# Half of one weight transfer cut into four 8-row pieces, each behind a tiny transfer, and 37 more filler products

## The chip, the cores and the metric

The kernel runs on one core of one Trainium2 chip. The metric is device time in microseconds (us), the median of several executions. A profile is one further execution. Its span (423.3 us for the kernel before) leaves out some 2 us that the device time has at its ends, so times on the profile's clock are compared only with one another. PE is the engine of the matrix products; its granted clock is the share of full speed at which it was allowed to run. POOL is the engine that issues the weight transfers, and the DMA share is the mean busy share of the core's sixteen DMA engines.

## The reference, cut to what matters

Linear attention makes `x`. A spectral step then mixes 64 frequencies of it, each with its own pair of 512 x 512 weight matrices, and a channel step ends it.

```python
def _moe_ref(x, w_r, w_i, w_ch):
    X = np.fft.rfft(x, axis=1)                       # x: 8 x 576 x 512
    Xr, Xi = (np.real(X[:, :64]), np.imag(X[:, :64]))
    Yr = np.einsum('bmd,mde->bme', Xr, w_r) - np.einsum('bmd,mde->bme', Xi, w_i)
    Yi = np.einsum('bmd,mde->bme', Xr, w_i) + np.einsum('bmd,mde->bme', Xi, w_r)
    ...                                              # the other frequencies are zero
    u = x + np.fft.irfft(Y, n=S, axis=1)
    return u + np.maximum(u @ w_ch, 0.0)
```

`w_r` and `w_i` hold 2 x 64 x 512 x 512 float32 values, 134 MB. The core reads all of them, each once, and that is the longest job of the kernel.

## The kernel before

The weights come in pairs of frequencies: pair p holds frequencies 2p and 2p+1. Each pair is two transfers issued from POOL, one from `w_r` and one from `w_i`, each of 64 rows of 32 KB. The transfer converts float32 to bfloat16, so a row is 16 KB on arrival (the trace of before has 16,384 bytes in a weight packet). Two buffers rotate. The last pair (31) comes in smaller pieces, so that little is left to do after the last one.

```python
    def w_load(p: int, half: int, pool, tag: str, bufs: int):
        if half == 0:
            w_in[p] = pool.tile([128, NDW, D], BF16, tag=tag, bufs=bufs, name=f"w{p}")
        two = (moe_w_r, moe_w_i)[half][2 * p : 2 * p + 2]
        pin(
            nc.gpsimd.dma_start(
                out=w_in[p][half::2], in_=two.rearrange("g (r dc) e -> (g r) dc e", dc=NDW)
            )
        )
    # ... cut: w_load_last, which loads pair 31 in pieces
```

`pin` keeps the written order of instructions. On PE each pair's products are followed by a number of fillers: products whose result nobody reads, there to keep the clock of PE up while it waits for weights.

```python
    def keep_warm(n: int):
        for _ in range(n):
            pin(nc.tensor.matmul(last_ps[0], id16, wch16[:, 0, :]))

    def mode_pair(p: int):
        # ... cut: the pair's products, their eviction and transposition
        keep_warm(FILL.get(p, 0))

    def last_pair():
        # ... cut: frequency 62
        keep_warm(6)
        kk = NM - 1
        y_last = psW.tile([128, NDC, 2 * B], F32, tag="P", bufs=2, name="y_last")
        # ... cut: 32 products with the last weights

    FILL = {**{p: 1 for p in range(20, 27)}, 27: 1, 28: 1, 29: 2, 30: 3}
```

## Time and profile before

| | before |
|---|---|
| median time, three runs | 424.95 us (424.81 to 425.3) |
| span of the profiled run, mean granted clock | 423.3 us, 0.788 |
| last landing of a weight | 389.70 us |
| from there to the end of the span | 33.6 us |

### The profile page before, as it was taken

What the parts mean: (1) busy time and instruction counts of PE and PEld (TensorE: products, weight loads), DVE (VectorE), ACT (ScalarE), POOL (GpSimd) and SP (SyncE); (2) the same over time, 40 slices, a digit from 0 to 9 for tenths busy, and PEclk for the clock granted to TensorE, in tenths of its full rate; (3) what the DMA queues carried; (4) which work ended last, traced back from release to release, by engine and by line L of the source; (5) the groups of instructions that cost most, each with busy time, mean ns of one, the idle gap of its engine ahead of it and who ended that gap; (6) DMA issues with size and microseconds to landing.
All of it is one profiled execution on the core that took longest, in us unless ns stands there. A gap on an engine that the chain in (4) does not pass through costs nothing.

```text
span 423.3 us, 7890 instructions
## 1 busy us (share of the span) xinstructions
PE 268.8 (63%) x3378; PEld 146.1 (35%) x3378; DVE 215.2 (51%) x447; ACT 161.4 (38%) x253; POOL 57.0 (13%) x99
## 2 busy tenths in 40 slices
PE   1358376778417645444344778869687785997992
PEld 0247355566202322222122323324243332463320
DVE  4599489994203453354444444445353424431793
ACT  4687588844202102000000244435253432330781
POOL 4222124210000100000000001100000000030000
PEclk9999889999755555555555598878898969899997
DMA  9999999999999999999999999999999999995697
GB/s 215 209 209 215 207 221 201 224 209 221 218 217 221 208 215 220 218 211 217 218 217 212 221 215 217 214 219 217 215 215 216 218 212 218 218 209 113 235 400 309
DMA packets 20802, 93.19 MB, mean 220 GB/s; under 512 B 2080, under 2 KB 11168, under 8 KB 16480
## 3 DMA queue, kind: packets, MB, share of 16 engines
q0 software_dynamic: 16512, 81.47, 93.8%
q1 hardware_dynamic: 4256, 11.22, 7.2%
q8 instruction: 26, 0.43, 0.4%
q14 instruction: 8, 0.07, 0.0%
HBM read 163.93 MB, written 9.44 MB: 410 GB/s over the span
## 4 chain that ended last, share of the span: by engine, by line
DMA 69%; PE 16%; DVE 4%; ACT 4%; issue 3%; POOL 2%; DVEq 0%; POOLq 0%; ACTq 0%
DMA w<-in_moe_w_i_dram 54%; DMA pick_sb<-row_pick 8%; PE P L442 7%; DMA k<-in_k_dram 7%; PE acc L735 3%; PE acc L774 2%; POOL w L119 2%; ACT ke L213 2%; ACT qT L249 1%; DVE ys L452 1%; DVE x L299 1%; PE yt L460 1%; ACT qe L213 1%; PE ya L653 0%; PE eps L676 0%
## 5 line engine op out<-in xcount | busy, mean ns | idle before, releaser
L442 PE MATMUL P<-w,xt_c 64*32 64x512 bf16 (+2 forms) x1000 | 51.7, 544 | 66.4 <-DMA w<-in_moe_w_i_dram 64.9
L452 DVE CAST ys<-P 128x512 f16<-128x512 f32 x32 | 22.1, 692 | 118.0 <-PE P L442 118.0
L454 ACT CAST ys<-P 128x512 f16<-128x512 f32 x31 | 18.2, 586 | 150.2 <-PE P L442 150.2
L119 POOL DMA_DIRECT2D w<-in_moe_w_r_dram x31 | 16.5, 534 | 245.1 <-PE P L442 105.9
L442 PEld LDWEIGHTS <-xt_c 64*32 64x32 bf16 (+2 forms) x1000 | 16.8, 128 | 84.7 <-DMA w<-in_moe_w_i_dram 51.1
L676 PE MATMUL eps<-wch,xTw 128*128 128x512 f16 x144 | 43.7, 434 | 0.0
L165 PEld LDWEIGHTS <-qT 64*128 64x128 f16 (+1 forms) x640 | 22.7, 123 | 52.9 <-issue 28.7
L657 DVE TENSOR_TENSOR x_main<-ya,x_main 128x512 f32<-128x512 f32 x32 | 22.0, 689 | 19.1 <-PE ya L653 18.9
L165 PE MATMUL num<-kv,qT 64*128 64x65 f16 (+1 forms) x320 | 13.4, 208 | 28.1 <-ACT kv L272 14.6
L659 ACT CAST x16w<-x_main 128x512 f16<-128x512 f32 x32 | 19.8, 618 | 25.0 <-DVE x_main L657 24.0
L684 ACT CAST E<-eps 128x512 f16<-128x512 f32 (+1 forms) x40 | 21.2, 541 | 11.2 <-PE eps L676 11.0
L165 PE MATMUL nw<-kv,qT 64*128 64x65 f16 (+1 forms) x320 | 19.0, 240 | 9.5 <-DVE x_tail L620 4.3
L460 PE MATMUL yt<-pick_sb,ys 128*128 128x16 f16 x252 | 11.7, 174 | 18.7 <-DMA pick_sb<-row_pick 12.1
L299 DVE TENSOR_TENSOR x<-num,rd 128x512 f16<-128x512 f32 x32 | 22.1, 692 | 1.1
L213 ACT ACTIVATE qe<-q 128x1152 f16<-128x1152 f16 (+1 forms) x16 | 17.8, 1156 | 10.5 <-DMA q<-in_q_dram 10.4
L249 ACT COPY qT<-qTp 128x1152 f16<-128x1152 f16 x16 | 19.7, 1298 | 0.2 <-PE qTp L242 0.2
L460 PEld LDWEIGHTS <-ys 128*128 128x128 f16 x252 | 9.7, 102 | 28.8 <-DVE ys L452 15.3
L242 PE MATMUL qTp<-id,qe 128*128 128x128 f16 x144 | 13.1, 264 | 10.0 <-DVE qe L226 9.5
L213 ACT ACTIVATE ke<-k 128x1152 f16<-128x1152 f16 x16 | 17.7, 1153 | 4.7 <-DMA k<-in_k_dram 4.7
L784 ACT ACTIVATE acc<-acc 128x512 f32<-128x512 f32 x34 | 18.1, 581 | 2.4 <-PE acc L735 1.5
L676 PEld LDWEIGHTS <-xTw 128*128 128x128 f16 x144 | 14.1, 110 | 12.6 <-issue 6.2
L119 POOL DMA_DIRECT2D w<-in_moe_w_i_dram x31 | 17.2, 555 | 4.8 <-DMA q<-in_q_dram 2.5
(114 smaller groups left out, 450.8 us busy)
## 6 DMA issues: line engine op xcount, KB each, us to landing
w<-in_moe_w_r_dram POOLq DMA_DIRECT2D x31, 1024.0 KB, 12.4
w<-in_moe_w_i_dram POOLq DMA_DIRECT2D x31, 1024.0 KB, 16.8
out_dram<-x_main SPq DMA_DIRECT2D x11, 512.0 KB, 4.8
k<-in_k_dram POOLq DMA_DIRECT2D x8, 576.0 KB, 12.7
v<-in_v_dram POOLq DMA_DIRECT2D x8, 576.0 KB, 14.8
q<-in_q_dram POOLq DMA_DIRECT2D x7, 576.0 KB, 12.7
out_dram<-x_main SPq DMA_DIRECT2D x6, 256.0 KB, 4.8
q<-in_q_dram SPq DMA_DIRECT2D x2, 576.0 KB, 4.4
```

Source lines behind the costliest of these rows:

```text
L119: nc.gpsimd.dma_start(out=w_in[p][half::2], in_=two.rearrange("g (r dc) e -> (g r) dc e", dc=NDW))
L165: mm = nc.tensor.matmul(num[hpo][orow, c0 : c0 + 65], qT[rows, hpp, h2, cols], kv_sb[rows, hpp, h2, :])
L213: pin(nc.scalar.activation(out=ev[:, c], in_=heads(nm, b, c), func=AF.Exp))
L249: nc.scalar.copy(out=qT[:, :, c * NJ : (c + 1) * NJ], in_=qT_ps.rearrange("p j x -> p x j"))
L299: nc.vector.tensor_tensor(out=dst.rearrange("p (o c d) -> p o c d", o=2, c=4), in0=nv[:, :, :, 0:64], in1=rden.unsqueeze(3).broadcast_to([ ...
L442: nc.tensor.matmul(P[c : c + n, :], xt_cols(dc, kk, n), w[rows, dc, :], start=(dc < NDC), stop=(dc >= n_dc - NDC), tile_position=(rows.sta ...
L452: pin(nc.vector.tensor_copy(out=st, in_=P))
L460: nc.tensor.matmul(yt_ps[:, ec, kk % 8, :], st[:, ec * 128 : ec * 128 + 128], pick_sb)
L657: pin(nc.vector.tensor_tensor(out=x, in0=acc, in1=x, op=ALU.add))
L659: pin(nc.scalar.copy(out=x16w[t], in_=x))
L676: nc.tensor.matmul(e_ps, xT[:, c, :], wch16[:, c, :], start=(c == 0), stop=(c == NDC - 1))
L684: pin(nc.scalar.copy(out=dst, in_=e_ps[:, cols]))
```

## The change

Eight of the sixteen DMA engines finish the weights some 3 us after the others (last landings of before at 388.36 to 389.70 us against 385.38 to 387.29). As I read the diff, the intent is to give the early half more rows of pair 20, so that all end together. Half of one transfer is sent as four transfers of 8 rows. The idea, as I read it, is that each of them goes to 8 engines and that the two halves take turns from one to the next; so a tiny transfer of 8 short rows stands before each, to use up the other half's turn. The fillers are set anew: 35 more behind the pairs from 20 on, and two more before the last products.

```diff
+    spare = const.tile([128, 2], F16, name="spare")[0:8]
 ...
+        rows_in = two.rearrange("g (r dc) e -> (g r) dc e", dc=NDW)
+        if (p, half) != (20, 0):
+            pin(nc.gpsimd.dma_start(out=w_in[p][half::2], in_=rows_in))
+            return
+        pin(nc.gpsimd.dma_start(out=w_in[p][half + 2 :: 4], in_=rows_in[1::2]))
+        for j in range(4):
+            for real in (0, 1):
+                if real:
+                    pin(nc.gpsimd.dma_start(out=w_in[p][half + 4 * j :: 16], in_=rows_in[2 * j :: 8]))
+                else:
+                    pin(nc.gpsimd.dma_start(out=spare, in_=moe_w_ch[0:8, 0:2]))
 ...
-        keep_warm(6)
+        keep_warm(8)
 ...
-    FILL = {**{p: 1 for p in range(20, 27)}, 27: 1, 28: 1, 29: 2, 30: 3}
+    FILL = {**{p: 4 for p in range(20, 27)}, 27: 7, 28: 1, 29: 8, 30: 5}
```

More of the change, by code (lines that the diff above doesn't have):

```diff
@@ L117, in w_load @@
         two = (moe_w_r, moe_w_i)[half][2 * p : 2 * p + 2]
-        pin(
-            nc.gpsimd.dma_start(
-                out=w_in[p][half::2], in_=two.rearrange("g (r dc) e -> (g r) dc e", dc=NDW)
-            )
-        )
+        rows_in = two.rearrange("g (r dc) e -> (g r) dc e", dc=NDW)
[9 more added lines that the diff above has]
+                    pin(nc.gpsimd.dma_start(out=spare, in_=moe_w_ch[0:8, 0:2]))
     def w_load_last(pool, tag: str, bufs: int):
```

## The prediction

The sum came to 424.95 + 6.4 - 0.55 = 430.8 us, less 0.5 for a shorter round trip: 430.3. The round trip of 2.6 us held 0.1 for waking POOL. The 6 and 2 rows an engine in (1), and with them the heavy and the light half in (2), are what the change intends if all four small transfers meet the same eight engines. That was assumed; the trace before does not show it.

> **What bounds the kernel now.** I read four views, in this order. First the page: its row of DMA shares and its chain that ended last.
>
> ```profile
> PEclk9999889999755555555555598878898969899997
> DMA  9999999999999999999999999999999999995697
> ...
> q0 software_dynamic: 16512, 81.47, 93.8%
> ...
> q8 instruction: 26, 0.43, 0.4%
> ...
> DMA 69%; PE 16%; DVE 4%; ACT 4%; issue 3%; POOL 2%; DVEq 0%; POOLq 0%; ACTq 0%
> ```
>
> The DMA engines are full from the first slice to the thirty-sixth; nine tenths of that is the queue that POOL issues to, which carries the weights. The chain is 69% DMA. Second, busy time by stage, around the end of the weights (columns: stretch, length, busy time and count of PE, PEld, DVE, ACT, POOL, then clock, DMA share, GB/s):
>
> ```profile
> 290.00:380.00 90.00, 71.89 (x739) 35.53 (x737) 36.56 (x69) 35.55 (x63) 12.17 (x23) 0.91 1.01 215
> 380.00:385.40 5.40, 3.81 (x35) 1.11 (x27) 0.69 (x1) 0.59 (x1) 0.00 (x0) 1.00 1.02 206
> 385.40:387.30 1.90, 1.90 (x16) 0.81 (x13) 1.32 (x2) 0.00 (x0) 0.00 (x0) 1.00 0.56 107
> 387.30:389.70 2.40, 1.74 (x31) 1.08 (x29) 0.00 (x0) 0.00 (x0) 0.00 (x0) 1.00 0.27 45
> 389.70:393.70 4.00, 3.60 (x20) 2.16 (x20) 1.09 (x3) 1.12 (x3) 0.33 (x1) 0.57 0.00 0
> ```
>
> The reader is to see that the share is full until 385.4 us and then falls in steps: about half the engines finish early while the rest work on. The trace keeps sixteen landings for each transfer, one an engine. Those of the very last weight piece are 385.38, .46, .63, .66, .81, 386.00, .17 (seven), 387.29 (one), 388.36, .54, .64, .69, .70, .76, .85 (seven) and 389.70. Eight engines are some 3 us behind. Why is in the trace too: the 25 instruction fetches of 16 KB before 389.7 (queue q8) take 0.89 to 0.98 us each, and their durations repeat with a period of eight, so they visit eight engines in turn, three each and a fourth for one. Third, the chain of waits at the end, and fourth, POOL's timeline where the changed load stands and at its last issue:
>
> ```profile
> 362.40 27.30 DMA w<-in_moe_w_i_dram x2
> 389.70 0.05 issue
> 389.75 0.30 PE y_last L504 x4
> 390.05 0.02 issue
> 390.07 0.24 DVE Y L510
> 390.31 0.05 issue
> 390.35 0.61 PE ypl L914 x4
> 390.96 0.85 PE zl L920 x4
> 391.81 0.85 PE z1l L920 x4
> ```
>
> ```profile
> 263.81 0.52 POOL L119 DMA_DIRECT2D w<-in_moe_w_r_dram  x1 [8.73 <-PE ya L653]
> 264.32 0.54 POOL L119 DMA_DIRECT2D w<-in_moe_w_i_dram  x1
> ...
> 393.37 0.57 POOL L929 DMA_DIRECT2D YZ_all<-last  x1 [15.62 <-ACT last L925]
> ```
>
> So everything waits for the last weight piece at 389.70, and what follows is a fixed tail of about 33 us. A transfer is 64 rows, four an engine; the trace's 16 KB packets (one row each) take 1.226 us, and the landings of successive transfers lie 4.85 us apart on each engine from start to end. There is no slack in this stream: any hole in it moves the end by its full length.
>
> [...] in an idle queue the issue at 393.37 had its first packet at 395.34 (1.97 us) and landed at 396.85 to 397.31. [...] a row's 32 KB read in 1.226 us is 26.7 GB/s,[...] a lone half gets no faster: the slow eight's steps over the last three small pieces are the fast eight's within 0.05 us. [...] stretches at half clock are multiples of 3.41 us, and one is 390.28 to 393.69, just behind the last weights.
>
> **The change part by part.** (1) Rows. Of pair 20's first transfer, half (32 rows) stays two an engine; the other 32 rows go as four transfers of 8 rows[...]. So eight engines get 6 rows, eight get 2: plus and minus 2 x 1.226 = 2.45 us. If the heavier half is the fast one, the ends become 387.8 to 388.6 for its seven, 389.74 for its eighth (387.29 + 2.45), and 385.9 to 387.25 for the others.
>
> (2) Waits, which the diff does not show and the built program does. All four tiny transfers write one tile, `spare`, so the second waits for the landing of the first, the third for the second, the fourth for the third: in the instruction order each carries a wait on the semaphore lane of the one before, at the count that includes it. POOL issues in order, so the real ones and the pair's second transfer stand behind these waits. The first tiny transfer lies in the queue behind pair 19 and the 32 rows. The slowest engine landed pair 19 at 272.05; plus 2.45 it reaches the tiny one at 274.5. At that moment the light half has nothing queued, and the heavy half only one row, which it has mostly finished. A round trip, by the issue at 393.37: 1.97 us to the first packet, about 0.5 from its end to the landing[...], so 2.6 (an estimate from that one transfer). Tiny issues then fall at 274.6, 277.2 and 279.8; the last real one at 280.3; the second transfer of the pair at 280.8, its packets from 282.8. Before, the slow engines started it at 275.1 to 276.5 (landings 275.49 to 276.90 less 0.4). The light half so loses 6.3 to 7.7 us. The heavy half gets its last row at 282.3 to 283.5 and goes on from there. All sixteen restart nearly together, so the old lag is wiped out whichever half was meant. From the end of that first transfer to the last landing an engine without fetches took 385.38 - 273.59 = 111.8 us, a fetching one 112.9. New end: heavy 283.9 + 111.8 to 112.3 = 395.7 to 396.2; light 283.2 + 112.9 = 396.1. Against 389.70: plus 6.4 us.
>
> (3) Eight more POOL issues of about 0.5 us: already inside (2).
>
> (4) 37 more fillers, 0.216 us apart at full clock: 8 us of PE, all behind waits for weights. The two added before y_last: the six end at 387.92, eight would end at 388.35, before y_last starts at 388.58. So no cost. Their possible gain: the window 386.86 to 390.28 held only about 1.1 us of streaming (columns over clock, added up from the trace) and was followed by half clock[...]. Two more fillers bring 1.5. With full clock ypl, zl and z1l (0.61 + 0.85 + 0.85) and the products after would take about 1.1 us less. But all of this moves by 6 us against the window's grid, so I count half: minus 0.55.[...]
>
> Sum: 424.95 + 6.4 - 0.55 = 430.8; as the round trip rests on one larger transfer and may be 2.3, I take off 0.5: 430.3 us.
>
> **Rivals.** (a) The balance works as meant and the waits cost nothing. The mean of the sixteen landings is 387.35, so 2.35 us is the most it can give; by (1) it gives 0 to 1.1, as the move overshoots. With the clock's 1.1: 422.8 to 425. For it: someone tuned these counts. Against it: three waits are in the built program, in a queue that is full before and empty behind them. (b) The heavy half is the slow one and there is no hole: 389.70 + 2.45 = 392.15, 427.4 us. (c) The hole is hidden by the load-ahead of two pairs. Against: at 263.81 the queue holds 5 to 8 us of work and the waits begin only when that is used up; PE waits for weights, never the other way for long. (d) A longer round trip, 3.3 us each, would bring 433.
>
> **Range and chances.** (2) dominates and I give it 85%: 428.5 to 432.5. Rivals (a) and (b) share the rest. Range 427.3 to 432.6. Over 2% slower needs 433.45, so rival (d): 8%. Over 2% faster needs 416.5, which no part can give: 1%.
>
> **What would show it.** Right: between about 274 and 283 us the DMA share falls well below 1; POOL has three issues spaced by 2.3 to 2.9 us ended by the landing of `spare`; the pair's second transfer is issued 15 us later than before; the last weights land near 396 with all engines within 1.5 us; the tail stays 33 us, less 1 if no half-clock window follows the last landing. Wrong: a DMA share of 1.0 through 270 to 290 and POOL issuing the nine transfers 0.5 us apart.

## More of the kernel before

One more view is needed to read the change: the busy time by stretch around the load that it touches. Its columns are the stretch, its length, busy time and count of PE, PEld, DVE, ACT and POOL, then the granted clock, the DMA share and GB/s.

```profile
270.00:274.00 4.00, 2.23 (x42) 1.40 (x42) 1.16 (x3) 1.02 (x2) 0.45 (x1) 1.00 0.96 205
274.00:276.00 2.00, 1.75 (x20) 0.80 (x19) 1.78 (x4) 1.23 (x3) 0.61 (x2) 1.00 1.08 229
276.00:278.00 2.00, 2.00 (x13) 0.79 (x11) 1.62 (x4) 1.08 (x2) 0.00 (x0) 1.00 1.04 221
278.00:283.00 5.00, 1.76 (x27) 0.61 (x33) 0.85 (x2) 1.72 (x3) 0.00 (x0) 0.80 1.02 218
```

The last but one column is what to read: the share is 1 throughout, give or take a few hundredths. The stream has no gap here, and POOL (the busy column with two and then no instructions) issues its next transfers long before they are needed.

## The result and the profile after

| | before | after |
|---|---|---|
| median time, same session | 424.88 us (423.82 to 425.3) | 431.11 us (430.43 to 431.35) |
| span of the profiled run, clock | 423.3 us, 0.788 | 428.6 us, 0.775 |
| last landing of a weight | 389.70 | 396.73 |
| from there to the end of the span | 33.64 | 31.90 |

All runs were fast (none more than 1.5% above the fastest of its kernel) and the results are right. The ratio is 1.0148 (95% interval 1.0126 to 1.017): 1.5% slower. Here and below a ratio is the mean time of one kernel's fast runs over the mean of the other's in the same rounds, so it is not quite the ratio of the medians in the table.

From the page of the kernel after, the row of DMA shares and the chain that ended last:

```profile
DMA  9999999999999999999999999579999999999697
...
DMA 65%; PE 19%; DVE 5%; ACT 4%; issue 3%; POOL 2%; DVEq 0%; POOLq 0%; ACTq 0%
```

The row of nines has a notch at the 26th and 27th of its forty slices, where before it had none. A slice is 10.7 us, so the notch lies at 268 to 289 us. Busy time by stretch shows the same four stretches as before:

```profile
270.00:274.00 4.00, 2.03 (x38) 1.06 (x38) 0.87 (x2) 0.59 (x1) 0.00 (x0) 0.94 0.52 107
274.00:276.00 2.00, 2.00 (x7) 0.44 (x6) 0.75 (x2) 1.09 (x2) 1.06 (x2) 0.50 0.08 16
276.00:278.00 2.00, 2.00 (x19) 1.06 (x17) 1.62 (x3) 0.88 (x3) 1.07 (x2) 0.76 0.46 66
278.00:283.00 5.00, 1.68 (x10) 0.64 (x9) 1.71 (x3) 2.16 (x4) 2.67 (x5) 1.00 0.50 80
```

The share fell from 1 to 0.52, 0.08, 0.46 and 0.50. Missing work, in units of the whole set of engines, is 4 x 0.44 + 2 x 1.00 + 2 x 0.58 + 5 x 0.52 = 7.5 us (share before less share after, times the length). Why the engines had nothing is in POOL's timeline (start, duration, engine, line, operation, tiles; in brackets the idle time before it and what ended that):

```profile
264.19 0.52 POOL L129 DMA_DIRECT2D spare<-in_moe_w_ch_dram  x1
264.70 0.58 POOL L127 DMA_DIRECT2D w<-in_moe_w_r_dram  x1
274.85 0.51 POOL L129 DMA_DIRECT2D spare<-in_moe_w_ch_dram  x1 [9.57 <-DMA spare<-in_moe_w_ch_dram]
275.35 0.56 POOL L127 DMA_DIRECT2D w<-in_moe_w_r_dram  x1
276.69 0.51 POOL L129 DMA_DIRECT2D spare<-in_moe_w_ch_dram  x1 [0.79 <-DMA spare<-in_moe_w_ch_dram]
277.19 0.57 POOL L127 DMA_DIRECT2D w<-in_moe_w_r_dram  x1
279.67 0.51 POOL L129 DMA_DIRECT2D spare<-in_moe_w_ch_dram  x1 [1.91 <-DMA spare<-in_moe_w_ch_dram]
280.17 0.56 POOL L127 DMA_DIRECT2D w<-in_moe_w_r_dram  x1
280.72 0.56 POOL L121 DMA_DIRECT2D w<-in_moe_w_i_dram  x1
```

Three of the four tiny transfers wait for the landing of the tiny one before, because all of them write the tile `spare`. POOL issues in order. So the last real piece stands behind three such waits, and so does the large transfer of the pair at 280.72, which before was issued at 264.32. The first wait, 9.57 us, is harmless for most of its length, since the queue still holds work; it harms from the moment the engines run out of it, one after another between 271 and 275 us.

At the end, the chain of waits of the kernel after answers to that shown of before:

```profile
370.48 26.25 DMA w<-in_moe_w_i_dram x2
396.73 0.05 issue
396.78 0.30 PE y_last L511 x4
...
397.38 0.40 PE ypl L921 x4
397.78 0.44 PE zl L927 x4
398.22 0.45 PE z1l L927 x4
```

The last landing is 7.03 us later. The three groups after it take 0.40, 0.44 and 0.45 us instead of 0.61, 0.85 and 0.85: the clock granted in the 4 us behind the last landing is 1.00 now, where it was 0.57. So the end moves by 7.03 - 1.74 = 5.3 us, the difference of the spans.

### The profile page after: what moved, and what is told of

It is laid out like the page before. It is cut to its first block, busy times and chain, and to the rows that moved or that the text cites. A ratio compares the mean times of both kernels' runs of the same rounds, so it can differ in the third digit from the quotient of the medians.

```text
span 428.6 us, 7976 instructions
## 1 busy us (share of the span) xinstructions
PE 280.2 (65%) x3415; PEld 153.6 (36%) x3415; DVE 215.3 (50%) x447; ACT 161.9 (38%) x253; POOL 60.7 (14%) x107
## 4 chain that ended last, share of the span: by engine, by line
DMA 65%; PE 19%; DVE 5%; ACT 4%; issue 3%; POOL 2%; DVEq 0%; POOLq 0%; ACTq 0%
DMA w<-in_moe_w_i_dram 47%; DMA pick_sb<-row_pick 8%; PE P L449 7%; DMA k<-in_k_dram 7%; DMA spare<-in_moe_w_ch_dram 3%; PE acc L742 3%; PE acc L781 2%; ACT ke L220 2%; PE eps L683 1%; POOL w L121 1%; DVE ys L459 1%; PE zl L432 1%; PE ya L660 1%; DVE x L306 1%; PE yt L467 1%
## 5 line engine op out<-in xcount | busy, mean ns | idle before, releaser
L683 PE MATMUL eps<-wch,xTw 128*128 128x512 f16 x144 | 42.7, 426 | 0.0
L249 PE MATMUL qTp<-id,qe 128*128 128x128 f16 x144 | 16.1, 301 | 10.0 <-DVE qe L233 9.4
L268 PE MATMUL kvp<-vpad,ke 64*128 64x130 f16 x288 | 14.7, 279 | 4.7 <-DVE vpad L239 2.9
## 6 DMA issues: line engine op xcount, KB each, us to landing
w<-in_moe_w_r_dram POOLq DMA_DIRECT2D x3, 512.0 KB, 10.7
```

What stands on the lines that cost most here:

```text
L683: nc.tensor.matmul(e_ps, xT[:, c, :], wch16[:, c, :], start=(c == 0), stop=(c == NDC - 1))
```

## The experiments

The theory: the loss is the round trips that the shared `spare` puts between POOL's issues, and nothing else of the change costs anything. Rivals: the split into 8-row pieces costs by itself; a new distribution of rows over the engines moves the end; the fillers cost time on PE. A second question was whether the tiny transfers do what they were put there for. Eleven kernels ran. All gave right results. Unless the diff says otherwise, they have the new fillers.

### Fillers alone

```diff
-        keep_warm(6)
+        keep_warm(8)
-    FILL = {**{p: 1 for p in range(20, 27)}, 27: 1, 28: 1, 29: 2, 30: 3}
+    FILL = {**{p: 4 for p in range(20, 27)}, 27: 7, 28: 1, 29: 8, 30: 5}
```

> The kernel before with the 37 fillers alone. Theory of the waits: the weights end as before (last landing near 389.7 us) and only the clock behind them changes; a full-clock tail makes 423.1 to 424.0 us, an unchanged one 424.9. Rival, the fillers cost the time: 428 or more.

Measured: 423.72 us (423.65 to 423.79) beside 424.94 of before, ratio 0.9982 (0.9964 to 0.9999). The last weight landed at 389.72, where it did before (389.70). The stretch of 4 us behind it, from busy time by stretch:

```profile
389.72:393.72 4.00, 3.44 (x39) 2.31 (x36) 1.90 (x4) 1.87 (x5) 0.57 (x1) 1.00 0.06 15
```

The clock is 1.00 there, where before it was 0.57 (prediction, last line of the second fence), and PE did 39 products instead of 20 in it. From the last landing to the end it took 32.14 us instead of 33.64. So the fillers cost nothing and bring something: 1.4 us between the two profiled spans, 0.8 us by the ratio of the timed runs. The two figures differ because the runs of the kernel before fall into two groups: of the eleven here, four took 423.52 to 424.01 us and seven 424.81 to 425.24. The profiled run of before (425.15 us) is of the upper group. All six runs with the new fillers took 423.65 to 423.79, close to the lower one. So the fillers seem to remove the slower group and not to make the faster one faster. That the slower group is the one with a stretch of half clock behind the last landing is likely, but no trace of a lower-group run of before was kept.

### The transfers alone, with the old fillers

```diff
     # the transfers of the change, and
     FILL = {**{p: 1 for p in range(20, 27)}, 27: 1, 28: 1, 29: 2, 30: 3}   # as before
         keep_warm(6)                                                        # as before
```

> The transfers of the change alone, with the old fillers. Theory of the waits: the last landing comes near 396.7 us as with the whole change, so 430.4 to 432 us, depending on the clock behind it. Rival, the fillers cost the time: near 425.

Measured: 432.73 us (431.76 to 433.41), 0.7 us above the expected range, ratio 1.0192 (1.0169 to 1.0215). The transfers thus carry the whole loss, and by these ratios the new fillers hide some of it: 1.0192 against 1.0148 of the whole change. In the profiled run the last landing is at 397.79, 1.06 us later than in the kernel after. There a second cause shows:

```profile
355.00:385.00 30.00, 24.16 (x199) 9.84 (x199) 8.97 (x15) 7.25 (x13) 2.17 (x5) 0.60 1.00 212
```

The granted clock is 0.60 for 30 us. PE falls behind, and the buffers come free later: the first transfer of the last pair is issued at 384.92, when the fastest engine had landed the transfer before (at 384.88) and so had nothing to do until the new one reached it. The DMA share of this run shows the second hole: 0.39 from 385 to 386 us and 0.80 from 386 to 387. So the fillers matter twice, once at the end and once for the time at which POOL may issue. That the low clock is why this issue came late is argued; no run isolates it.

### A place of its own for each tiny transfer

```diff
-    spare = const.tile([128, 2], F16, name="spare")[0:8]
+    spare = const.tile([128, 2], F16, name="spare")
-                    pin(nc.gpsimd.dma_start(out=spare, in_=moe_w_ch[0:8, 0:2]))
+                    pin(nc.gpsimd.dma_start(out=spare[8 * j : 8 * j + 8], in_=moe_w_ch[0:8, 0:2]))
```

The four places are slices of one tile. They don't overlap, so none waits for another.

> The whole change, but each tiny transfer writes its own eight partitions of the spare tile, so none waits for the one before. Waits for a free semaphore lane remain from the third real transfer on; the last of them ends near 274.5 us. Theory of the waits: the hole of 273 to 283 us shrinks to at most 2 us, and 4 to 5 of the 6 us come back: 425.5 to 427.4 us, with the last landing near 392[...]. Rival, the rows themselves cost it (the heavier half is overloaded): stays at 430 to 431. Rival, balance as intended: 423 or below.

Measured: 425.78 us (425.24 to 427.33), ratio 1.0037 (1.0016 to 1.0057). Most of the loss is gone. What is left is in POOL's timeline (of the slowest of the six runs, 427.33 us; the others took 425.24 to 426.78):

```profile
266.55 0.51 POOL L129 DMA_DIRECT2D spare<-in_moe_w_ch_dram  x1
267.54 0.57 POOL L127 DMA_DIRECT2D w<-in_moe_w_r_dram  x1 [0.48 <-DMA w<-in_moe_w_r_dram]
272.36 0.51 POOL L129 DMA_DIRECT2D spare<-in_moe_w_ch_dram  x1 [4.25 <-DMA w<-in_moe_w_i_dram]
275.44 0.56 POOL L127 DMA_DIRECT2D w<-in_moe_w_r_dram  x1 [2.57 <-DMA w<-in_moe_w_r_dram]
275.99 0.55 POOL L121 DMA_DIRECT2D w<-in_moe_w_i_dram  x1
```

No issue waits for `spare` any more, but the last three of the nine still wait for earlier weight transfers. The built program has eight semaphores for POOL's transfers and takes them in turn (in the traces of before and after, numbers 99 to 106 over POOL's 95 and 103 issues), and each of these three issues waits for the transfer issued eight before it, whose semaphore it is to use again: the two of the pair before and, for the last real piece, the first transfer of this pair, which landed at 275.16. So cutting one transfer into nine brings a second wait of its own, and a smaller hole: the DMA share is 0.19 in 274 to 276 us and 0.81 in 276 to 278. The last landing is at 391.94, 2.2 us behind that of the fillers alone.

### The four pieces without tiny transfers

```diff
+        pin(nc.gpsimd.dma_start(out=w_in[p][half + 2 :: 4], in_=rows_in[1::2]))
+        for j in range(4):
+            pin(nc.gpsimd.dma_start(out=w_in[p][half + 4 * j :: 16], in_=rows_in[2 * j :: 8]))
```

> The whole change without the four tiny transfers: the four real ones then go to the two halves in turn, so every engine gets four rows as before, in five transfers in place of one. Theory of the waits: no hole, last landing at 389.7 to 390.2 us, 423.1 to 425.2 us. Rival, small transfers of 8 partitions are slow in themselves: 427 or more.

Measured: 424.21 us (423.54 to 424.73), ratio 0.9991 (0.9974 to 1.0008). The last landing is at 389.85, and every engine got four rows. By the ratios, five transfers in place of one cost 0.4 us against the fillers alone, and the intervals overlap. The rival "the split costs by itself" is out.

### The waits without the split

The transfer goes whole; four tiny ones, all into one place, stand between it and the pair's second transfer.

```diff
+        pin(nc.gpsimd.dma_start(out=w_in[p][half::2], in_=rows_in))
+        for j in range(4):
+            pin(nc.gpsimd.dma_start(out=spare, in_=moe_w_ch[0:8, 0:2]))
```

> The waits alone: pair 20's first transfer whole as before, then the four tiny transfers into the one spare tile, then the pair's second transfer; fillers as in the change. Theory of the waits: the first tiny one lands near 277 us, three round trips of 1.9 us each and the issue follow, so the second transfer starts near 282.5 instead of 275 to 276.5, last landing near 395.5, 429 to 430.5 us. Rival, the hole comes from splitting the rows: 423.5 to 425.

Measured: 431.63 us (431.39 to 432.26), 1.1 us above the expected range, ratio 1.017 (1.0149 to 1.0192). POOL's timeline:

```profile
265.32 0.52 POOL L125 DMA_DIRECT2D spare<-in_moe_w_ch_dram  x1
277.46 0.50 POOL L125 DMA_DIRECT2D spare<-in_moe_w_ch_dram  x1 [11.63 <-DMA spare<-in_moe_w_ch_dram]
279.29 0.51 POOL L125 DMA_DIRECT2D spare<-in_moe_w_ch_dram  x1 [1.33 <-DMA spare<-in_moe_w_ch_dram]
281.30 0.50 POOL L125 DMA_DIRECT2D spare<-in_moe_w_ch_dram  x1 [1.50 <-DMA spare<-in_moe_w_ch_dram]
281.78 0.55 POOL L121 DMA_DIRECT2D w<-in_moe_w_i_dram  x1
```

With no row moved to another transfer, the waits alone bring back the whole loss. This run measures the round trip as well, in an empty queue: 279.29 - 277.46 = 1.83 and 281.30 - 279.29 = 2.01 us from one tiny issue to the next, of which 1.55 and 1.73 are from issue to the last of the sixteen landings. The first packets moved 1.11 to 1.13 us after these issues.

### Two places for four tiny transfers

```diff
+                    pin(nc.gpsimd.dma_start(out=spare[j % 2 * 8 : j % 2 * 8 + 8], in_=moe_w_ch[0:8, 0:2]))
```

> The whole change with two spare places in place of one: the third tiny transfer waits for the first, the fourth for the second, so one round trip of the three is left. Theory of the waits: between one place and four: the pair's second transfer is issued near 277, one us later than with four places and four us earlier than with one; last landing near 393, 426 to 428 us. Rival, any wait costs the same whatever the number: 430 to 431.

Measured: 429.17 us (428.21 to 432.33) beside 425.21, ratio 1.0112 (1.0083 to 1.0141). It lies between the kernel after and the four places, as it should, but above the range expected. The transfers do what was expected of them; POOL's timeline has one wait for `spare` where the kernel after has three:

```profile
275.29 0.51 POOL L129 DMA_DIRECT2D spare<-in_moe_w_ch_dram  x1 [7.79 <-DMA spare<-in_moe_w_ch_dram]
...
277.50 0.56 POOL L121 DMA_DIRECT2D w<-in_moe_w_i_dram  x1
```

The last landing is at 394.33, half way between 391.94 and 396.73. The profiled run lost more at its end, as its chain of waits shows:

```profile
394.35 2.01 PE zl L432 x8
396.36 0.92 PE y_last L511 x32
```

L432 is the filler. When the last weights landed, PE was behind, and the eight fillers that should fill its wait stood in its way: the last products ended 2.93 us after the landing instead of 0.33. The clock was 0.71 from 360 to 380 us, against 0.83 in the kernel after. This profiled run was the slowest of six (432.33 us; the others 428.21 to 430.3), so it shows what can happen and not how much of it every run has. Its trace says why PE was behind: the granted clock never rose above 0.85 in the whole execution, where each of the other twelve profiles reaches 1.00. So this end belongs to that execution and not to the two places. The other five runs are above the expected range too; the last landing, 1.3 us later than expected, is part of that, and the rest stays open.

### What the five kernels have in common

For the kernels with a hole, the issue of the pair's second transfer and the last landing, both read from the traces (in us):

| kernel | second transfer issued | last landing | between |
|---|---|---|---|
| four places | 275.99 | 391.94 | 115.95 |
| two places | 277.50 | 394.33 | 116.83 |
| after | 280.72 | 396.73 | 116.01 |
| transfers alone, old fillers | 280.84 | 397.79 | 116.95 |
| waits without the split | 281.78 | 397.64 | 115.86 |

The end of the weights follows the time of that issue, and next to nothing else. The two that lie 0.8 to 1.1 above the others have reasons of their own: in the second row the last two real pieces are issued one straight after the other, so two of them stand in the queue ahead of the large transfer, which landed 9.30 us after its issue instead of 7.94 to 8.28; in the fourth, the late issue near the end described above.

### Do the tiny transfers shift the rows?

The trace has every packet with its start and duration, to a nanosecond, and on a full queue each packet starts within some 0.02 us of where that engine's last one ended, so each engine's packets can be strung together. In the run with four places, the first real piece of 8 rows went to eight engines, the second to the other eight and the third to the first eight again, though a tiny transfer stood before each. The fourth met an empty queue, where packets can't be strung. All four tiny transfers went to one and the same half, that of the first and third pieces. So the tiny ones did not move the turn on, and the real pieces were spread over both halves. I tried to make a real shift with other transfers.

Two kernels cut the last 16 rows of the transfer so that of each row 1 KB and 15 KB go in separate transfers, which then take the place of the tiny ones:

```diff
+        load(slice(0, 48), every)
+        for r in (slice(48, 56), slice(56, 64)):
+            load(r, some)      # 1 of 16 parts of a row; in the other kernel load(r, rest) comes first
+            load(r, rest)
```

> A balance without waits and without tiny transfers: 48 rows in one transfer, the other 16 rows as two groups of 8, each group first 512 columns (a sixteenth), then the other 7680 columns. If a transfer of 8 partitions moves the round of engines on by eight, both wide parts meet the half of the engines that the first 8-partition transfer does not meet, and that half gets about 0.9 rows (1.1 us) more, the other as much less. By my reading of the landings that half holds six of the eight lagging engines: last landing near 390.8 in place of 389.7, 424 to 425.5 us with the fillers' gain. Rival, as the author meant it, that half is the fast one: last landing 388.6, 422.6. Rival, the narrow ones do not move the round: wide ones alternate, 389.7, 423.7.

> The mirror: in each group of 8 rows the wide part first, then the narrow one, so the half that the first 8-partition transfer meets gets 1.1 us more. It holds two lagging engines and the six of the others: last landing 389.8 to 390.8 where one of these two has the most fetches, the spread of the sixteen under 3 us; 423.5 to 424.8 us. Rival, this half is the lagging one as a whole: last landing 390.8 and a spread of over 5 us.

Measured: 424.33 us (423.65 to 425.88), ratio 1.0002 (0.9981 to 1.0023), and 424.09 us (423.55 to 426.12), ratio 0.9998 (0.9975 to 1.002). Last landings 389.95 and 390.00. By the packets (1,024 bytes in a narrow part, 15,360 in a wide one) all four parts, narrow and wide, went to the same eight engines in both orders, and none to the others. So rows were shifted, five on each of these eight engines and three on each of the others, but not in the way expected: none of the parts used up a turn, as a tiny transfer doesn't either. As I read the landings, the heavier half held most of the engines that finish early and two that finish late. Neither time is better than that of the fillers alone. A third kernel put a transfer of 14 rows ahead, meant to turn the start of the round by 14:

```diff
+        load(slice(1, 64, 2), every)
+        load(slice(0, 28, 2), every)
+        for r in (slice(32, 48, 2), slice(48, 64, 2)):
+            load(r, rest)
+            load(r, some)
+        load(slice(28, 32, 2), every)
```

> A version meant to beat both: 32 rows in one transfer, 14 rows in a 14-partition transfer[...], then two groups of 8 rows, wide part first, then a 2-partition transfer[...]. If the lagging eight are consecutive engines as I infer, they are just the eight that the wide parts now miss: fast ones end at 386.5 to 388.4, lagging ones at 387.3 to 388.6, last landing 388.4 to 388.7 and a spread under 2.5 us; with the fillers 422.2 to 423 us. Rival, the inference is wrong: last landing 389.8 to 391, 423.7 to 425.

Measured: 424.2 us (423.62 to 424.92), ratio 0.9993 (0.9974 to 1.0013), last landing 390.16. The four parts were again all on one half, and the transfer of 14 rows had met that half too; the expectation failed, and with it my picture of where the round starts. Two more kernels asked whether the half follows from which rows a transfer takes instead of from a turn:

```diff
+        for r in (slice(1, 64, 2), slice(2, 64, 4), slice(0, 64, 8), slice(4, 64, 8)):   # groups_0_2
+        for r in (slice(1, 64, 2), slice(0, 64, 4), slice(2, 64, 8), slice(6, 64, 8)):   # groups_1_3
+            pin(nc.gpsimd.dma_start(out=wp[r], in_=rows_in[r]))
```

> No tiny transfers, no waits: 48 rows in two transfers over all engines, then two groups of 8 rows, those at rows 0 and 4 of each eight. Theory A, each 8-partition transfer moves the round of engines on by eight: one group to each half, all engines get four rows, the sixteen last landings as before (385.4 to 389.8, seven under 386.5). Theory B, the half follows from where the rows lie and not from what went before (these two met the same half whatever stood between): one half gets 1.2 us more, the other as much less; two engines land near 384.3 to 385.2, the rest later than before by 1.2 or nearer together. Time 423.5 to 425 in both.

> The same with the groups at rows 2 and 6 of each eight. Theory A: as before, 385.4 to 389.8. Theory B: both meet the other half, which holds six lagging engines: five or six engines land near 384.3 instead of 385.5, six near 389.9, the last near 390.8; spread over 6 us; 424.3 to 425.5 us.

Measured: 424.24 us (423.62 to 424.86), ratio 0.9983 (0.9965 to 1.0001), and 424.04 us (423.53 to 424.81), ratio 0.9981 (0.9964 to 0.9999). The sixteen landings of the last piece are 385.69 to 387.39 (eight) and 388.65 to 390.01 (eight) in the one, 385.75 to 387.65 (eight) and 388.69 to 390.11 (eight) in the other: those of the kernel before within some 0.4 us, with no row moved. So for these pieces of whole rows the half follows a turn, which two such transfers one after the other use up, and not the rows.

What stays open: why some transfers of 8 rows take turns and others always meet the same half, and what decides which half that is. Those that took turns carried whole rows to partitions 16 apart; those that didn't carried a part of each row (4 bytes, 1 KB or 15 KB) to partitions 1 to 4 apart, and no run separates the two. The time of the change does not hang on it, as the table above shows. No version beat the fillers alone clear of noise; they beat both kernels by the ratios.

## Why the prediction was right

The time came out at 431.11 us against 430.3, inside the range, and for the reason given. Point by point:

- **What bounds the kernel** held. The stream lost 7.5 us of work in the hole, and the last landing came 7.03 us later.
- **Step (1), the rows, was wrong.** It assumed that with a tiny transfer before each of them all four real pieces meet the same half of the engines, which no trace had shown. They don't: in the run with four places all four tiny ones met one half, and the real pieces alternated. No engine of the kernel after can have got six rows or two, as the second and the third real piece met different halves there too. The prediction did not suffer, since step (2) said that the hole wipes out the old lag whichever half was meant. It did: the landings of the last piece lie within 2.0 us (394.72 to 396.73) instead of the 4.3 us of before. Predicted were 1.5.
- **Step (2), the waits, held nearly to the tenth.** First tiny landing 274.56 (predicted 274.5), last real issue 280.17 (280.3), second transfer of the pair 280.72 (280.8). Single round trips were mis-sized: 2.6 us predicted; 1.84 and 2.98 in the kernel after, and 1.83 and 2.01 in the empty queue of the run with the waits alone. The one of 2.98 is longer because the third tiny transfer stands behind a row of a real piece on eight engines: it landed at 278.20 to 278.29 on eight and at 278.82 to 279.14 on the others. The errors have opposite signs, and with the first wait ending 0.25 us later than predicted the sum came out right (last tiny issue 279.67, predicted 279.8); that was luck. The 2.6 us came from a wrong reading: the issue at 393.37 did not meet idle engines, since SP's half of that store was moving from 394.38 to 395.5, so its 1.97 us to the first packet are too long. The tiny ones took 1.11 to 1.13 us to the first packet. From the landing of one to the issue that waited for it the kernel after took 0.28 to 0.53 us (274.56 to 274.85, 276.41 to 276.69, 279.14 to 279.67). Since the round trips were right in sum, the 0.5 us taken off at the end for a shorter one was wrong: the landing moved by 7.03 us, where the sum had 6.4 - 0.5 = 5.9. The remaining 0.6 is the stretch from the issue at 280.7 to the end, 116.0 us instead of the 396.1 - 280.8 = 115.3 us that the prediction came to.
- **Step (3)**, eight more issues, held: they are inside the waits.
- **Step (4), the fillers, was mis-sized.** Their cost of nothing held. Their gain was worked out as 1.1 us, and then halved to 0.55 because the grid might fall otherwise (in the traces of before and after, the stretches of one clock between two changes last multiples of 3.41 us). The tail became 1.74 us shorter. The first `acc` comes 1.05 us earlier after the last landing (2.38 against 3.43 us), which is the clock. The other 0.69 lies behind it, mostly in the stores; the profiled run of before had an instruction fetch of 1.65 us among its first stores and that of after had none of that length (whether that is the reason was not tried). The profiled run of before is of its slower group, so 1.74 is the gain against that group alone; over all timed runs the fillers bring 0.8 us, nearer to the 0.55.
- So the sum was 5.9 - 0.55 = 5.35 by the prediction and 7.03 - 1.74 = 5.3 in the profiles: two terms, each 1.1 to 1.2 us too small in size, cancelled, which was luck as well. In the timed runs, where the profiled run of after was the fastest of four, the medians differ by 6.2, which is 7.03 less those 0.8.
- **Rivals.** (a), the balance works and the waits cost nothing, fell with the kernel after; (b), no hole, fell with the DMA share of 0.08; (c), hidden by loading ahead, fell with the run of the waits alone; (d), a longer round trip, fell with the measured 1.8 to 3.0 us.

How the change divides, by the ratios: fillers 0.9982, so about -0.8 us of 425; the rest is 1.0148 - 0.9982 = 0.0166, about 7.1 us, and of that the four places take away 1.0148 - 1.0037 = 0.0111, about 4.7 us, which is therefore the share of the common `spare`. The other 0.0055, about 2.3 us, I put down to the waits for the eight semaphores that the run with four places shows; that was not tried by itself.

## What to carry to other kernels

A transfer that nobody reads still has a destination. Here those that wrote the same destination waited for each other's landing, and as POOL issued in order, everything behind stood still for a round trip each (1.83 to 2.98 us from one tiny issue to the next, once the first had landed). So give each its own place, and count the transfers against the semaphores that rotate: with nine transfers against eight of them, three issues still waited 0.48, 4.25 and 2.57 us. Before splitting a transfer in a full stream, ask at which moment the queue runs dry and what stands between that moment and the next large issue: here that one time fixed the end to within 1.1 us. Judge a bundle of changes in its parts: the fillers alone were worth keeping, and they hid part of what the other half lost.
